# Splitting the first ten weight tiles during the first routing, and subtracting low parts in four pieces

## The chip, the cores and the metric

The kernel runs on one core of a Trainium2 chip. The metric is the time of one execution in microseconds (us); the kernel before takes 1088.62 us in the median of three runs (1088.23 to 1089.11). The engines are named as in the profile: PE (TensorE) multiplies, DVE (VectorE), ACT (ScalarE) and POOL (GpSimd) work elementwise, and SP, ACT and POOL start DMA transfers. Each engine works through its own queue in order.

## The reference, cut to what matters

Three stages follow each other. A linear attention gives 3072 rows of 512 numbers. A router spreads the rows over 8 experts, at most 384 rows each, greedily by score, and each expert is a two-layer network. A last network, the same for all rows, has an ELU between two wide layers:

```python
h = np.maximum(x[mask] @ w1[e], 0.0)      # expert e, 512 -> 1024
out[mask] = h @ w2[e]                     # 1024 -> 512
h = x @ w_in                              # all rows, 512 -> 2048
g = np.where(h > 0.0, h, alpha * (np.exp(np.minimum(h, 0.0)) - 1.0))
return (g @ w_out).astype(np.float32)     # 2048 -> 512
```

## The kernel before

The attention runs first (to about 136 us of the profiled execution). The router then finds the rows of the first expert (phase 0, about 138 to 168 us): a search that goes back and forth between DVE and PE, level after level, since each level's result picks the next level's thresholds. Then the experts follow one by one. Expert n has 8 chunks of L1 and of L2 (its own network) and 16 chunks of F1 and of F2 (the last network on its 384 rows). The order of the chunks is the list `seq`, and `prep` gets a chunk's weights ready three chunks ahead. The router's search for the next expert runs in pieces between them, so DVE's queue in an expert is a fixed mixture of ELU steps, conversions and search steps.

Products are made to full precision from parts: each matrix is a high part (rounded) and a low part (the rest), and three products are added. The tiles of `w_in` and `w_out`, 16 each of 128x512, come as 64-bit numbers. `Wide.chunks` turns each into a 32-bit tile by two DVE operations (L252, L253), an ACT operation (L255) and a POOL addition (L259); `wide.step` runs the next third of that. Thirty such steps run in the attention, which completes ten tiles, w_in and w_out in turn, five of each. The other 22 follow while expert 0 is computed (`CONV`, `n == 0`).

`Wide.parts` gives a chunk's high and low part. On the first call for a tile ACT writes the high part (L272), and POOL subtracts it from the tile (L275: one operation of 128x512), and the low part goes to DRAM through SP's queue (L276); the high part stays on the chip. On later calls the low part is read back by SP (L268). The calls come from `prep`, so all 32 subtractions run in the F1 and F2 chunks of expert 0 (about 216 to 334 us), and experts 1 to 7 only read back. Low parts have three buffers (`LOWS`) for w_in (`wis`) and three for w_out (`wos`); the pools of high parts hand out two spare tiles first and then the tiles of converted weights from the first on, so a high part may wait for an older tile's subtraction.

Of the kernel before, what the change touches and what calls it, by code (L numbers as in the profile page):

```python
# [10 lines left out]
F32 = mybir.dt.float32  # L11
# [189 lines left out]
class Paced:  # L201


    def __init__(self, eng):
        self.eng, self.free, self.now = eng, 0.0, lambda: 0.0
# [13 lines left out]
class Wide:  # L219
# [6 lines left out]
    def __init__(self, nc, tc, ctx, a):  # L226
        self.nc, self.a = nc, a
        self.pools = [ctx.enter_context(tc.tile_pool(name=n, bufs=16 + MORE)) for n in ("win", "wout")]
        self.raw = [[p.tile([128, 512], F32, name="w") for _ in range(16)] for p in self.pools]
        self.low = nc.dram_tensor("low", (2, 16, 128, 512), F32, kind="Internal").ap()  # L230
        self.high = {}
        self.sb = ctx.enter_context(tc.tile_pool(name="wsb", bufs=STAGES))
        self.loaded, self.stage, self.steps = 0, {}, self.chunks()

    def load(self):
# [10 lines left out]
    def chunks(self):  # L246
        V = self.nc.vector
        for i in range(32):
            t = self.stage.pop(i)
            lo, hi = t[:, 0:1024:2], t[:, 1:1024:2]  # L250
            m = self.raw[i % 2][i // 2].bitcast(I32)
            V.tensor_scalar(m, hi, 3, 0x3FFFFFFF, op0=OP.logical_shift_left, op1=OP.bitwise_and)  # L252
            V.scalar_tensor_tensor(m, hi, -0x40000000, m, op0=OP.bitwise_and, op1=OP.bitwise_or)  # L253
            yield
            self.nc.scalar.activation(lo, lo.bitcast(U32), AF.Copy, scale=2.0 ** -29)  # L255
            if i:
                self.load()
            yield
            self.nc.gpsimd.tensor_tensor(m, m, lo, OP.add)  # L259
            yield  # L260

    def parts(self, which, f, pool, later):


        nc, name = self.nc, ("wis", "wos")[which]
        lo = pool.tile([128, 512], F32R, name=name, bufs=LOWS)
        if (which, f) in self.high:
            nc.sync.dma_start(lo.bitcast(F32), self.low[which, f])  # L268
            return self.high[which, f], lo
        hi = self.high[which, f] = self.pools[which].tile([128, 512], F32R, name="w")  # L270
        src = self.raw[which][f]
        nc.scalar.activation(hi, src, AF.Copy)  # L272

        def low():
            nc.gpsimd.tensor_sub(lo, src, hi.bitcast(F32))  # L275
            nc.sync.dma_start(self.low[which, f], lo.bitcast(F32))  # L276

        later(low)
        return hi, lo
# [305 lines left out]
def mlps(nc, tc, ctx, a, xd, out, router, wide, ident, acc, rot, pms):  # L585

    sb = ctx.enter_context(tc.tile_pool(name="sb", bufs=2))
# [6 lines left out]
    def gather_w(n, which, pair):  # L594
        t = sb.tile([128, 1024], F32, name="s" + which)
        nc.gpsimd.indirect_dma_start(  # L596
            out=t, out_offset=None, in_=a[f"{which}_{pair}"],
            in_offset=bass.IndirectOffsetOnAxis(ap=router.es[n][:, :1], axis=0))
        WS[n, which, pair] = t

    def gather_x(n, tb):
        t = sb.tile([128, DM], F32, name="row", bufs=4)
        nc.gpsimd.indirect_dma_start(
            out=t, out_offset=None, in_=xd,
            in_offset=bass.IndirectOffsetOnAxis(ap=router.idx[n][:, tb:tb + 1], axis=0))
        XG[n, tb] = t
# [21 lines left out]
    def tick(us):  # L628

        clock[0] += us  # L630
        while heap and heap[0][0] <= clock[0]:
            heapq.heappop(heap)[2]()
# [155 lines left out]
    def advance(i):  # L788

        while ahead[0] <= min(i, len(seq) - 1):  # L790
            kind = seq[ahead[0]][0]
            if sum(ck[0] == kind for ck in WSP) == ROOM[kind]:
                return
            prep(seq[ahead[0]])
            ahead[0] += 1
# [2 lines left out]
        return acc.tile([128, 512], F32, name="acc")[:, :384]  # L798

    router.spare = spare  # L800
    for _ in router.phase(0):
        tick(1.0)
        if 0 in router.es and (0, "w1", 0) not in WS:
            gather_w(0, "w1", 0)
            gather_w(0, "w2", 0)
        if 0 in router.idx and (0, 0) not in XG:
            for tb in range(3):
                gather_x(0, tb)
            advance(1)
# [45 lines left out]
def body(ctx, tc, a, xd, out):  # L855
# [33 lines left out]
    pms = ctx.enter_context(tc.tile_pool(name="pms", bufs=1, space=PSUM))  # L889

    mlps(nc, tc, ctx, a, xd, out, router, wide, ident, acc, rot, pms)


# [87 lines left out]
```

## Time and profile before

| what | value |
|---|---|
| median of 3 runs | 1088.62 us |
| the profiled execution: its own time | 1088.59 us |
| its span, first to last instruction | 1086.8 us |
| busy: PE, DVE, POOL, ACT | 998.1, 741.5, 406.3, 350.3 us |
| chain that ended last: PE, DVE, the rest | 72%, 18%, 10% |

A page lists for each engine how long it was busy, in which parts of the span, and which group of instructions (a line, an operation, its tiles) cost how much. A table by stretches gives the same for chosen windows of time. A time line gives single instructions with start and duration; behind some of them stands how long the engine had been idle before, and for whom it waited. An instruction's duration holds any time in which it had started but could not get on.

### The profile page before, as it was taken

What the parts mean: (1) busy time and instruction counts of PE and PEld (TensorE: products, weight loads), DVE (VectorE), ACT (ScalarE), POOL (GpSimd) and SP (SyncE); (2) the same over time, 40 slices, a digit from 0 to 9 for tenths busy, and PEclk for the clock granted to TensorE, in tenths of its full rate; (3) what the DMA queues carried; (4) which work ended last, traced back from release to release, by engine and by line L of the source; (5) the groups of instructions that cost most, each with busy time, mean ns of one, the idle gap of its engine ahead of it and who ended that gap; (6) DMA issues with size and microseconds to landing.
All of it is one profiled execution on the core that took longest, in us unless ns stands there. A gap on an engine that the chain in (4) does not pass through costs nothing.

```text
span 1086.8 us, 20264 instructions
## 1 busy us (share of the span) xinstructions
PE 998.1 (92%) x7730; PEld 896.0 (82%) x7730; DVE 741.5 (68%) x2294; ACT 350.3 (32%) x712; POOL 406.3 (37%) x412
## 2 busy tenths in 40 slices
PE   8888947987689999999999999999999999999995
PEld 6877825876578988998899888988998898999994
DVE  4566677989998877887787788777977513431431
ACT  3343403343344323332343233323332332233221
POOL 4555406766666320622071217021702182027001
PEclk9899959888889999999999999999999999999998
DMA  9788506346434263426432633264227426332441
GB/s 366 252 303 299 192 27 205 109 151 203 174 117 146 68 204 118 137 77 213 124 130 68 226 116 115 78 225 123 99 88 225 124 89 203 123 109 87 126 127 49
DMA packets 68194, 163.43 MB, mean 150 GB/s; under 512 B 8832, under 2 KB 15616, under 8 KB 68096
## 3 DMA queue, kind: packets, MB, share of 16 engines
q1 hardware_dynamic: 49712, 99.04, 27.7%
q0 software_dynamic: 13056, 46.14, 12.6%
q10 hardware_dynamic: 5328, 16.94, 4.6%
q8 instruction: 61, 1.00, 0.4%
q14 instruction: 37, 0.30, 0.1%
HBM read 141.13 MB, written 20.97 MB: 149 GB/s over the span
## 4 chain that ended last, share of the span: by engine, by line
PE 72%; DVE 18%; issue 3%; POOL 2%; DMA 2%; ACT 1%; POOLq 0%; ACTq 0%; DVEq 0%
PE pr L670 10%; PE pr L672 10%; PE pr L671 10%; PE acc L748 8%; PE acc L750 7%; PE acc L749 7%; DVE scr L215 3%; PE py L138 3%; PE acc L670 3%; PE acc L671 3%; PE acc L672 3%; PE pq L107 2%; DVE w L253 2%; DVE Tb L215 2%; DVE candf L215 2%
## 5 line engine op out<-in xcount | busy, mean ns | idle before, releaser
L670 PE MATMUL pr<-yh,w 128*128 128x384 f32 x512 | 179.4, 350 | 1.7 <-DVE ni L215 1.1
L672 PE MATMUL pr<-yh,wis 128*128 128x384 f32 x512 | 175.2, 342 | 0.0
L671 PE MATMUL pr<-yl,w 128*128 128x384 f32 x512 | 173.9, 340 | 0.1
L662 POOL TENSOR_TENSOR w1l<-sw,w1h 128x512 fp32r<-128x512 f32 x56 | 73.1, 1305 | 250.0 <-ACT w1h L659 233.3
L748 PE MATMUL acc<-w,gh 128*128 128x512 f32 x384 | 158.1, 412 | 0.0
L750 PE MATMUL acc<-w,gl 128*128 128x512 f32 x384 | 154.0, 401 | 3.3 <-DVE gl L215 3.3
L749 PE MATMUL acc<-wos,gh 128*128 128x512 f32 x384 | 154.2, 402 | 0.0
L596 POOL DMA_INDIRECT sw<-in_w,es x64 | 66.3, 1036 | 190.7 <-DVE es L215 142.3
L736 ACT ACTIVATE gh<-g 128x384 fp32r<-128x384 f32 x128 | 67.2, 525 | 181.5 <-DVE g L215 181.5
L215 DVE TENSOR_SCALAR_CACHE_REDUCE scr<-vt,candf 128x192 bf16<-128x192 f32 x350 | 124.3, 408 | 1.8
L729 ACT ACTIVATE g<-pr 128x384 f32<-128x384 f32 x128 | 62.8, 490 | 181.2 <-PE pr L672 173.1
L215 DVE TENSOR_SCALAR g<-g 128x384 f32<-128x384 f32 x128 | 49.2, 385 | 83.9 <-ACT g L729 82.3
L670 PEld LDWEIGHTS pr<-yh,w 128*128 128x128 f32 x512 | 98.2, 192 | 7.7 <-issue 2.7
L671 PEld LDWEIGHTS pr<-yl,w 128*128 128x128 f32 x512 | 98.1, 192 | 4.5 <-issue 0.4
L672 PEld LDWEIGHTS pr<-yh,wis 128*128 128x128 f32 x512 | 97.8, 191 | 0.0
L215 DVE TENSOR_TENSOR gl<-g,gh 128x384 fp32r<-128x384 f32 x128 | 77.4, 605 | 25.7 <-ACT gh L736 24.4
L750 PEld LDWEIGHTS acc<-w,gl 128*128 128x128 f32 x384 | 73.8, 192 | 22.1 <-DVE gl L215 4.6
L672 PE MATMUL pr<-xh,w1l 128*128 128x384 f32 x256 | 87.1, 340 | 4.0 <-POOL w1l L662 3.9
L670 PE MATMUL pr<-xh,w1h 128*128 128x384 f32 x256 | 88.1, 344 | 1.5 <-ACT w1h L659 1.5
L670 PE MATMUL acc<-hh,w2h 128*128 128x384 f32 x256 | 88.1, 344 | 0.0
L748 PEld LDWEIGHTS acc<-w,gh 128*128 128x128 f32 x384 | 73.6, 192 | 16.1 <-issue 2.4
L671 PE MATMUL acc<-hl,w2h 128*128 128x384 f32 x256 | 86.2, 337 | 0.4 <-DVE hl L215 0.4
(187 smaller groups left out, 2096.1 us busy)
## 6 DMA issues: line engine op xcount, KB each, us to landing
wis<-low SPq DMA_DIRECT2D x112, 256.0 KB
wos<-low SPq DMA_DIRECT2D x112, 256.0 KB, 2.7
Q<-in_kq SPq DMA_DIRECT2D x15, 768.0 KB, 5.8
V<-in_kv SPq DMA_DIRECT2D x15, 768.0 KB, 10.0
stg<-in_w_in ACTq DMA_DIRECT2D x16, 512.0 KB, 3.9
stg<-in_w_out ACTq DMA_DIRECT2D x16, 512.0 KB, 5.5
x_rows<-xs SPq DMA_DIRECT2D x32, 192.0 KB, 8.7
low<-wis SPq DMA_DIRECT2D x16, 256.0 KB, 2.0
```

Source lines behind the costliest of these rows:

```text
L138: nc.tensor.matmul(p[h, pr, :], q[r, n, pr], v[r, n, pr], start=True, stop=True)
L215: return getattr(self.eng, name)(*args, **kw)
L596: nc.gpsimd.indirect_dma_start(out=t, out_offset=None, in_=a[f"{which}_{pair}"], in_offset=bass.IndirectOffsetOnAxis(ap=router.es[n][:, :1 ...
L662: (V if (kind, f) in BYV else nc.gpsimd).tensor_sub(lo, src, hi.bitcast(F32))
L670: nc.tensor.matmul(p, ah, bh, start=first, stop=False)
L671: nc.tensor.matmul(p, ah, bl, start=False, stop=False)
L672: nc.tensor.matmul(p, al, bh, start=False, stop=last)
L729: nc.scalar.activation(g, p, AF.Exp)
L736: at(ELU[0], lambda: nc.scalar.activation(gh, g, AF.Copy))
L748: nc.tensor.matmul(p, gh[:, s], wh, start=f == 0, stop=False)
L749: nc.tensor.matmul(p, gh[:, s], wl, start=False, stop=False)
L750: nc.tensor.matmul(p, gl[:, s], wh, start=False, stop=f == 15)
```

## The change

The converter counts its finished tiles in `wide.done`. In the loop over the first routing, each of the first ten turns calls `parts` for one finished tile, w_in and w_out in turn, and runs its subtraction and its store at once. When expert 0 asks for these ten tiles, `parts` now finds the high part and reads the low part back from DRAM. And every subtraction, early or not, is four POOL operations of 128x128 in place of one of 128x512.

```diff
@@ Wide.chunks
             self.nc.gpsimd.tensor_tensor(m, m, lo, OP.add)
+            self.done = i + 1
             yield
@@ Wide.parts
         def low():
-            nc.gpsimd.tensor_sub(lo, src, hi.bitcast(F32))
+            for c in range(0, 512, 128):
+                s = slice(c, c + 128)
+                nc.gpsimd.tensor_sub(lo[:, s], src[:, s], hi[:, s].bitcast(F32))
             nc.sync.dma_start(self.low[which, f], lo.bitcast(F32))
@@ mlps
     router.spare = spare
+    early = iter(range(wide.done))
     for _ in router.phase(0):
         tick(1.0)
+        i = next(early, None)
+        if i is not None:
+            wide.parts(i % 2, i // 2, sb, lambda low: low())
         if 0 in router.es and (0, "w1", 0) not in WS:
```

PE and DVE get the same rows in the same order as before. Lines behind the insertions move on by one to four (L275 becomes L279, L259 becomes L260, L268 becomes L270, L276 becomes L280).

POOL's queue between the attention's last scaling (`tabk`) and the gathers of expert 0's weights (`es0`), before and after; in a row stand line, operation, what is written and read, and the size:

```order
L259 TENSOR_TENSOR w_88<-w_88,stg_1734 128x512
L115 TENSOR_TENSOR V3_144<-V3_144,tabk_146 64x256 x2
L596 DMA sw1_2560<-in_w1_0,es0_2557 128x1024
L596 DMA sw2_2562<-in_w2_0,es0_2557 128x1024
L603 DMA row_2654<-x_rows,idx0_2652 128x512
```

```order
L115 TENSOR_TENSOR V3_144<-V3_144,tabk_146 64x256 x2
L279 TENSOR_TENSOR wis_2269<-w_68,w_2270 128x128 x4
L279 TENSOR_TENSOR wos_2302<-w_84,w_2303 128x128 x4
L279 TENSOR_TENSOR wis_2313<-w_69,w_2314 128x128 x4
L279 TENSOR_TENSOR wos_2323<-w_85,w_2324 128x128 x4
L279 TENSOR_TENSOR wis_2342<-w_70,w_2343 128x128 x4
L279 TENSOR_TENSOR wos_2375<-w_86,w_2376 128x128 x4
L279 TENSOR_TENSOR wis_2386<-w_71,w_2387 128x128 x4
L279 TENSOR_TENSOR wos_2396<-w_87,w_2397 128x128 x4
L279 TENSOR_TENSOR wis_2411<-w_72,w_2412 128x128 x4
L279 TENSOR_TENSOR wos_2444<-w_88,w_2445 128x128 x4
L600 DMA sw1_2640<-in_w1_0,es0_2637 128x1024
```

Forty pieces now stand between the two, ahead of the gathers.

POOL's queue where expert 0's F1 chunks begin, before and after:

```order
L275 TENSOR_TENSOR wis_3239<-w_68,w_3240 128x512
L275 TENSOR_TENSOR wis_3264<-w_69,w_3265 128x512
L259 TENSOR_TENSOR w_92<-w_92,stg_3143 128x512
L275 TENSOR_TENSOR wis_3306<-w_70,w_3307 128x512
L275 TENSOR_TENSOR wos_3309<-w_84,w_3310 128x512
L259 TENSOR_TENSOR w_77<-w_77,stg_3198 128x512
L275 TENSOR_TENSOR wis_3339<-w_71,w_3340 128x512
```

```order
L260 TENSOR_TENSOR w_92<-w_92,stg_3223 128x512
L260 TENSOR_TENSOR w_77<-w_77,stg_3278 128x512
L260 TENSOR_TENSOR w_93<-w_93,stg_3349 128x512
L260 TENSOR_TENSOR w_78<-w_78,stg_3398 128x512
L279 TENSOR_TENSOR wis_3546<-w_73,w_3547 128x128 x4
L260 TENSOR_TENSOR w_94<-w_94,stg_3446 128x512
L279 TENSOR_TENSOR wis_3632<-w_74,w_3633 128x128 x4
```

The additions of the conversion now stand alone until the sixth tile of w_in (w_73).

SP's queue at the same chunks, before and after (`low` is the copy in DRAM):

```order
L276 DMA low<-wis_3239 128x512
L276 DMA low<-wis_3264 128x512
L276 DMA low<-wis_3306 128x512
L276 DMA low<-wos_3309 128x512
L276 DMA low<-wis_3339 128x512
```

```order
L280 DMA low<-wos_2444 128x512
L270 DMA wis_3319<-low 128x512
L270 DMA wis_3341<-low 128x512
L270 DMA wis_3380<-low 128x512
L270 DMA wos_3382<-low 128x512
L270 DMA wis_3407<-low 128x512
L270 DMA wos_3439<-low 128x512
```

Ten stores moved into the routing, and ten reads stand where they were.

## Rows read from the trace of the kernel before

**Rows 1.** Table by stretches (us): busy time and instructions per engine, PE clock, DMA
```profile
138.30:156.00 17.70, 7.52 (x176) 6.24 (x177) 11.79 (x56) 0.00 (x0) 0.00 (x0) 0.50 0.01 2
172.00:216.00 44.00, 36.98 (x286) 32.98 (x285) 37.05 (x60) 15.04 (x30) 31.43 (x24) 0.92 0.47 156
216.00:254.00 38.00, 33.11 (x195) 27.95 (x193) 32.85 (x64) 17.70 (x35) 23.90 (x18) 0.91 0.48 159
254.00:334.00 80.00, 58.57 (x271) 50.73 (x272) 75.79 (x160) 29.43 (x60) 52.03 (x40) 0.84 0.44 155
453.00:560.00 107.00, 106.00 (x587) 96.26 (x586) 86.18 (x330) 34.33 (x70) 32.82 (x33) 1.00 0.42 133
```

**Rows 2.** Time line: one DVE step with no POOL work beside it
```profile
291.44 0.69 DVE L253 SCALAR_TENSOR_TENSOR w<-stg,w 128x512 int32<-128x512 int32 x1
```

**Rows 3.** Time line: a POOL subtraction and the same DVE step beside it
```profile
296.80 1.49 POOL L275 TENSOR_TENSOR wis<-w 128x512 fp32r<-128x512 f32 x1
297.16 1.68 DVE L253 SCALAR_TENSOR_TENSOR w<-stg,w 128x512 int32<-128x512 int32 x1
```

**Rows 4.** Time line of DVE, 216 to 333: rows stretched beside subtractions
```profile
216.91 1.84 DVE L253 SCALAR_TENSOR_TENSOR w<-stg,w 128x512 int32<-128x512 int32 x1
226.14 1.46 DVE L215 TENSOR_SCALAR g<-g 128x384 f32<-128x384 f32 x1
228.84 3.13 DVE L215 TENSOR_TENSOR cmp<-v,cand 128x372 bf16<-128x372 f32 x2
252.69 1.11 DVE L215 TENSOR_TENSOR tot<-CG,rem 128x8 f32<-128x8 f32 x1
332.34 1.71 DVE L215 TENSOR_TENSOR gl<-g,gh 128x384 fp32r<-128x384 f32 x1
```

**Rows 5.** Time lines of PE and DVE: waits for each other in this stretch
```profile
219.27 0.44 PE L671 MATMUL acc<-hl,w2h 128*128 128x384 f32 x1 [0.42 <-DVE hl L215]
245.43 0.17 DVE L215 TENSOR_REDUCE ni<-pm 128x1 int32<-128x8 f32 x1 [0.68 <-PE pm L401]
```

**Rows 6.** Time lines: POOL operations back to back, and DVE rows beside the smaller ones
```profile
29.17 5.41 POOL L115 TENSOR_TENSOR V<-V,tabk 64x256 f32<-64x256 f32 x8
349.62 1.30 POOL L662 TENSOR_TENSOR w2l<-sw,w2h 128x512 fp32r<-128x512 f32 x1
350.86 1.31 POOL L662 TENSOR_TENSOR w1l<-sw,w1h 128x512 fp32r<-128x512 f32 x1
26.40 0.98 DVE L253 SCALAR_TENSOR_TENSOR w<-stg,w 128x512 int32<-128x512 int32 x1
54.40 0.79 DVE L215 TENSOR_TENSOR cmp<-v,jb 128x186 bf16<-128x186 f32 x1
84.10 0.34 DVE L215 TENSOR_TENSOR cmp<-v,jb 128x186 bf16<-128x186 f32 x1
```

**Rows 7.** Time line of DVE: one level of the search in phase 0
```profile
142.85 0.17 DVE L215 TENSOR_REDUCE ni<-pm 128x1 int32<-128x8 f32 x1 [0.28 <-PE pm L401]
143.28 1.00 DVE L215 TENSOR_TENSOR cmp<-v,cand 128x372 bf16<-128x372 f32 x2
144.39 0.19 DVE L215 TENSOR_TENSOR pre<-jb,Tb 128x31 int32<-128x31 int32 x1
144.85 0.24 DVE L215 TENSOR_SCALAR_CACHE_REDUCE sat<-pm,remp 8x31 bf16<-8x31 f32 x1 [0.28 <-PE pm L395]
145.38 0.17 DVE L215 TENSOR_REDUCE ni<-pm 128x1 int32<-128x8 f32 x1 [0.28 <-PE pm L401]
```

**Rows 8.** Time line of DVE: a step of one number per row, stretched
```profile
350.22 3.22 DVE L215 SCALAR_TENSOR_TENSOR Tb<-ni,Tb 128x1 int32<-128x1 int32 x1
```

**Rows 9.** Time lines of POOL and ACT after phase 0's search; the page's DMA issues
```profile
160.11 1.14 POOL L596 DMA_INDIRECT sw<-in_w,es  x1 [29.68 <-DVE b L215]
164.73 1.15 ACT L659 ACTIVATE w1h<-sw 128x512 fp32r<-128x512 f32 x2 [28.77 <-DVE ga L215]
wos<-low SPq DMA_DIRECT2D x112, 256.0 KB, 2.7
```

More of the change, by code (lines that the diff above doesn't have):

```diff
@@ L232, in __init__ @@
         self.sb = ctx.enter_context(tc.tile_pool(name="wsb", bufs=STAGES))
+        self.done = 0
         self.loaded, self.stage, self.steps = 0, {}, self.chunks()
```

## The prediction

> **What bounds the kernel now.** I read the table by stretches first. From 453 to 560 us, a later expert, PE is busy 106 of 107 us at full clock. Expert 0 is different: from 216 to 334 us DVE is busy 108.6 of 118 us while PE has gaps and a clock of 0.84 to 0.91 [rows 1]. Since PE and DVE wait for each other only in short spells there, whatever makes DVE's queue shorter in this stretch makes the kernel shorter, until PE is next.
>
> The time line then shows that much of DVE's busy time is not work. The step of line L253 takes 0.69 us with POOL quiet [rows 2], and 1.68 us when a subtraction of POOL began just before [rows 3]: 0.99 us are lost, and the step ends 0.55 us after POOL's. DVE steps that read PSUM keep their length beside POOL; those with two inputs on the chip, and plain scalar steps, stretch. I walked through DVE's rows from 216 to 334 us and gave what each takes above its undisturbed length to the POOL operation it overlaps: the 32 subtractions cost DVE about 25.5 us, 0.80 us each (the first and the last such row, and three between, in [rows 4]); POOL's other operations cost some 14 us more. The other place that matters is phase 0. There DVE and PE wait for each other in turn, one level taking 2.53 us [rows 7], and POOL and ACT are idle for 29.68 and 28.77 us before their next work [rows 9].
>
> **The change part by part.** *Ten subtractions leave expert 0.* Beside them stand nine stretched DVE rows, from 216.91 to 252.69 us [rows 4]. Their excess is 1.15, 1.01, 1.12, 0.31, 2.13 (a pair that takes 1.00 undisturbed [rows 7]), 0.53, 0.64, 0.33 and 0.94, together 8.16 us. Not all of it arrives. The first row holds up PE by 0.42 us only [rows 5], so 0.73 of it is swallowed by PE's own run of L2. From 238 to 246 us DVE waits three times, 1.63 us together, the longest 0.68 us for PE [rows 5]; these waits grow first. I take 8.16 - 0.73 - 1.63 = 5.8 us as the gain; the ends are 3 us, if the waits take up about half of the rest as well, and all 8.2 us.
>
> *Forty pieces enter phase 0.* Cost of a piece on POOL: eight operations of 256 columns take 5.41 us, 0.68 each, and one of 512 columns follows the next by 1.24 us [rows 6]. So 256 columns are 0.56 us, and a piece of 128 takes 0.40 us; four take 1.60 in place of 1.24. How long a piece stops a DVE step is not in the trace. An operation of 512 stopped one for 0.99 us [rows 2, 3]; one of 256 stopped a step for 0.45 us (0.79 against 0.34) and another for 0.29 (0.98 against 0.69) [rows 2, 6]. The line through 0.99 and 0.45 gives 0.18 us at 128; a quarter of 0.99 is 0.25. I take 0.18, since the two smaller rows lie below proportion on average.
>
> In those rows with 256 columns DVE came in between two operations of a run, so I let a piece and a DVE step take turns. A level has five steps that a piece can stop: `cand`, two `cmp`, `Tb` and `pre`. DVE has no such step from the end of `pre` (144.58) to the end of the next `ni` (145.55), which takes two or three pieces free of charge; one piece before each of the five steps makes 7.5 per level. On the path lie `cand` and both `cmp`, 3 x 0.18 = 0.54 us. Pieces before `Tb` and `pre` push `sat` by 0.36 less the 0.28 us that it waits for PE anyway [rows 7], 0.08. So a level costs 0.62 us. The first level has four such steps on the path, 0.72 us, and takes about eight pieces; the other 32 need 4.3 levels, 2.7 us. Phase 0 grows by 3.4 us. From below: the pieces stop DVE for at most 40 x 0.18 = 7.2 us in all, and DVE is idle 5.9 of 17.7 us [rows 1], which leaves 1.3. From above with 0.25: 4 x 0.25 + 4.3 x (0.75 + 0.22) = 5.2 us.
>
> POOL should be through by about 157 us, ahead of the gather that comes at 160.11 and moves later by the same 3.4 us [rows 9]. If the pieces ran past it, every microsecond would delay the first weights.
>
> *22 subtractions are cut in four.* They keep 17.3 us of the 25.5, 0.79 each, which is 80% of the 0.99 that a full stop costs. Four pieces stop DVE for 4 x 0.18 x 0.8 = 0.58 us: 22 x 0.21 = 4.6 us gained. Against that, five of the 22 follow directly on a gather of POOL, and the DVE step that met the gather lost the whole run behind it; the run is now 0.36 us longer, 1.8 us. Net gain 2.8 us. Ends: at 0.25 per piece the cut gains nothing and costs the 1.8; if pieces meet a step that they can stop only half the time, it gains 22 x (0.79 - 0.36) = 9.5 less 1.8.
>
> *At nothing:* ten rounding steps of ACT move from a stretch in which it is busy 17.7 of 38 us [rows 1] into its idle time. Ten stores of SP move into phase 0, and ten reads of the same size take their place; a read lands in 2.7 us [rows 9], is queued three chunks ahead, and experts 1 to 7 live on such reads. In SP's queue the stores of later tiles now stand behind reads that wait for a free buffer; what those stores hold up is the buffer of the third tile after. If that cover went, F1 would wait up to 2.7 us for a tile. POOL's extra 22 x 0.36 = 7.9 us fall into a stretch where it is busy 52 of 80 [rows 1].
>
> **Sum.** 1088.59 us of the profiled execution (the median is 1088.62) + 3.4 - 5.8 - 2.8 = 1083.4 us.
>
> **The rivals.** *A, no change.* A piece costs 0.25. Then phase 0 grows by 5.2, the cut gains 0 and gives back 1.8, and 5.8 are saved: 1089.8 us. For it speaks that the step at 54.40 lost 0.45 of a pitch of 0.68, about the same share as at 512; against it the 0.29.
>
> *B, slower.* The port that both need is held for the whole reading of a piece, 0.28 us by the slope in [rows 6]. Place: the search of phase 0, where each of the three steps of a level waits for one piece. Price: 4 x 0.28 + 4.3 x (0.84 + 0.28) = 5.9 us there, 22 x (0.90 - 0.79) = 2.4 and 1.8 in expert 0, less 5.8: 1092.9 us. It decides from about 0.25 us per piece on.
>
> *C, slower by more.* The four pieces of a run don't let DVE in. One row looks like this: a step on one number per row took 3.22 us [rows 8], through three operations of POOL that stood back to back, two of them in [rows 6]. Then phase 0 grows by 40 x 0.40 - 5.9 = 10.1 us, and each kept tile costs 0.36 x 0.8 more, 6.3 us: 1099.2 us. Against it: at 216.91 DVE came in between two subtractions that stood back to back.
>
> *D, the whole piece.* A piece stops DVE for its whole 0.40 us. Phase 0: 4 x 0.40 + 4.3 x (1.20 + 0.52) = 9.0; expert 0: 22 x (1.28 - 0.79) + 1.8 = 12.6; less 5.8: 1104.4 us. The Trainium skill has this as a rule (SBUF — State Buffer, Who interferes with whom): whichever of the two starts first keeps the shared pair of ports for its whole instruction, and the other blocks. The trace agrees that the loser waits, but not on the length: 0.99 of 1.24 us and 0.45 of 0.68, so it has a small chance.
>
> *E, faster by more.* All 8.2 us arrive, phase 0 grows by 1.3, and the cut gains 9.5 - 1.8: 1074.0 us. For it: fewer gaps would also raise PE's clock, 0.84 from 254 to 334 us [rows 1].
>
> **How the numbers follow.** Chances: forecast 0.50 (its own range 1080 to 1086), A 0.22, B 0.10, C 0.06, D 0.03, E 0.09. The range from 1077 to 1094 us holds the forecast, A and B and leaves out C, D and E, 0.18. About 0.2% (2.2 us) is what a measurement of this kernel can tell from no change: faster is the forecast and E, 0.59; the same is A, 0.22; slower are B, C and D, 0.19.
>
> **What would show it right or wrong.** In the profile of the changed kernel: a level of the search of 3.0 to 3.3 us while POOL's pieces run, and 2.5 after them; phase 0's first gather 3 to 4 us later than 160.11; DVE rows of L253 beside pieces below 1.1 us on average; the stretch from the first L1 product to the last F2 product of expert 0 shorter by 8 to 9 us; later experts at 107 us as before. It is wrong if the level grows by over 1 us (B, C, D), if the pieces are still running when the gather is due, if DVE rows are stopped through whole runs of pieces (C), or if PE waits for a low part that comes from DRAM.

## The result, and the profile after

The changed kernel takes 1076.47 us in the median of four runs (1072.23 to 1078.40), the kernel before 1088.42 beside it. The ratio is 0.9891, 95% interval 0.9855 to 0.9927: 11.9 us faster, where 5.2 us were forecast. Two repetitions on other occasions gave 0.9897 (0.9860 to 0.9933) and 0.9874 (0.9843 to 0.9906). The profiled execution took 1078.40 us, its span is 1076.6 us.

The table by stretches of the changed kernel comes first, to be set against [rows 1]: length, busy time and instructions of PE, PE's weight loads, DVE, ACT and POOL, then PE's granted clock, DMA share and GB/s.

```profile
138.20:159.40 21.20, 7.68 (x175) 6.25 (x176) 17.21 (x56) 2.87 (x6) 19.61 (x40) 0.53 0.31 120
178.00:221.80 43.80, 36.51 (x274) 32.96 (x273) 34.51 (x59) 14.40 (x28) 27.54 (x22) 0.88 0.42 143
221.80:252.50 30.70, 29.64 (x193) 25.86 (x192) 25.24 (x60) 12.62 (x25) 12.32 (x14) 1.00 0.47 147
252.50:323.80 71.30, 54.99 (x271) 47.28 (x270) 67.31 (x160) 28.38 (x58) 61.46 (x96) 0.90 0.51 173
442.80:549.80 107.00, 106.00 (x587) 96.26 (x586) 86.18 (x330) 34.30 (x70) 32.83 (x33) 1.00 0.42 133
```

Later experts are as before: 106.00 of 107 us of PE in the last row, to the digit, and from the first output row of expert 0 to the end both kernels take 747.6 us. All of the difference lies in front of that. In the stretch that held 195 products in 38 us there are now 193 in 30.7, with PE busy 29.6 of them. In the next one, 271 products took 80 us and take 71.3. DVE has the same 160 instructions there, and 67.31 us in place of 75.79. POOL, with 61.46 of 71.3 us, has little room left.

To see where each microsecond went I cut every trace at the same six rows. These are the time lines' rows of the changed kernel: the last product of the attention, POOL's first gather for expert 0, the first `hh` of L1, the first and the sixth ELU step `g` of F1, and the first output row of expert 0.

```profile
135.93 0.64 PE L171 MATMUL pL<-wg,xT 128*64 128x8 f32 x16 [0.18 <-ACT xT L162]
162.82 1.13 POOL L600 DMA_INDIRECT sw<-in_w,es  x1 [4.69 <-DVE pos L215]
178.45 0.49 ACT L688 ACTIVATE hh<-pr 128x384 fp32r<-128x384 f32 x1 [2.43 <-PE pr L676]
230.29 0.49 ACT L733 ACTIVATE g<-pr 128x384 f32<-128x384 f32 x1 [1.05 <-PE pr L676]
251.25 0.49 ACT L733 ACTIVATE g<-pr 128x384 f32<-128x384 f32 x1
329.01 0.59 ACT L761 ACTIVATE row<-acc 128x512 f32<-128x512 f32 x1
```

The same rows in the kernel before; its first gather starts at 160.11 us [rows 9]:

```profile
136.01 0.64 PE L171 MATMUL pL<-wg,xT 128*64 128x8 f32 x16 [0.18 <-ACT xT L162]
175.05 0.49 ACT L684 ACTIVATE hh<-pr 128x384 fp32r<-128x384 f32 x1 [2.43 <-PE pr L672]
225.18 0.49 ACT L729 ACTIVATE g<-pr 128x384 f32<-128x384 f32 x1
252.77 0.47 ACT L729 ACTIVATE g<-pr 128x384 f32<-128x384 f32 x1
339.19 0.59 ACT L757 ACTIVATE row<-acc 128x512 f32<-128x512 f32 x1
```

The stages between these rows, for all kernels of the study (experiments below), stand in the next table in us. The ratio sets a kernel against executions of the kernel before beside it. Gains in us below are this ratio times the time of the kernel before, about 1086 us; plain differences of the medians depart from them by up to 2.4 us.

| kernel | last pL to gather | gather to first hh | first hh to g 1 | g 1 to g 6 | g 6 to output row | ratio to before |
|---|---|---|---|---|---|---|
| before | 24.10 | 14.94 | 50.13 | 27.59 | 86.42 | 1 |
| changed | 26.89 | 15.63 | 51.84 | 20.96 | 77.76 | 0.9891 |
| changed, repeated | 26.84 | 15.70 | 48.67 | 20.94 | 77.75 | 0.9897 |
| changed, third time | 26.86 | 15.60 | 51.84 | 20.96 | 77.85 | 0.9874 |
| e1, move, no cut | 30.77 | 15.74 | 50.38 | 22.63 | 85.75 | 1.0001 |
| e3, move, cut in phase 0 alone | 26.84 | 15.75 | 49.50 | 22.62 | 85.83 | 0.9975 |
| e4, move, cut in expert 0 alone | 30.78 | 15.73 | 48.82 | 20.94 | 77.85 | 0.9919 |
| e2, cut, no move | 24.08 | 15.01 | 49.61 | 24.51 | 78.82 | 0.9919 |
| e2, repeated | 24.06 | 15.11 | 49.75 | 24.52 | 78.00 | 0.9876 |
| two pieces | 26.66 | 15.76 | 51.77 | 21.78 | 81.76 | 0.9932 |
| eight pieces | 26.89 | 15.78 | 49.43 | 20.94 | 84.69 | 0.9991 |
| additions cut too | 26.88 | 15.82 | 51.95 | 20.04 | 80.80 | 0.9902 |
| attention's additions cut | 26.69 | 15.88 | 51.57 | 20.94 | 77.82 | 0.9876 |
| no subtraction of the 22 | 26.86 | 15.70 | 51.68 | 20.94 | 64.85 | 0.9754 |

Three of the five columns repeat to 0.3 us where the program is the same there, and the column behind g 6 to 0.1 us in the changed kernel and to 0.8 in e2. So one profile of each kernel is enough to read them. The column from the first hh to g 1 doesn't repeat: 51.84, 48.67 and 51.84 us for one program. Nor does the end of the attention, which lay between 131.8 and 138.9 us in the 14 profiles. These two are large enough for most of the 6 to 10 us by which single executions differ, and no difference in them is ascribed to the change. For the end of the attention this was tried (below). For the other column it is open: six of the nine profiles with pieces in phase 0 have 51.6 to 52.0 us there, the other five profiles 48.8 to 50.4.

From the kernel before to the changed one the table says: +2.8 and +0.7 up to the first hh, -6.6 from g 1 to g 6, -8.7 behind it; together -11.8 us, close to the 11.9 us of the medians. The two profiled executions themselves differ by 10.2 us, since the changed one took 1.7 us more from the first hh to g 1.

### The profile page after: what moved, and what is told of

The parts are those of the page before. It is cut to its first block, busy times and chain, and to the rows that moved or that the text cites. A ratio compares the mean times of both kernels' runs of the same rounds, so it can differ in the third digit from the quotient of the medians.

```text
span 1076.6 us, 20354 instructions
## 1 busy us (share of the span) xinstructions
PE 992.8 (92%) x7730; PEld 891.6 (83%) x7730; DVE 732.7 (68%) x2294; ACT 350.5 (33%) x712; POOL 424.3 (39%) x508
## 4 chain that ended last, share of the span: by engine, by line
PE 71%; DVE 19%; issue 3%; POOL 3%; DMA 2%; ACT 1%; another core or an unknown queue 0%; POOLq 0%; SPq 0%; DVEq 0%; ACTq 0%
PE pr L674 10%; PE pr L676 10%; PE pr L675 10%; PE acc L752 8%; PE acc L753 7%; PE acc L754 7%; DVE scr L215 3%; PE acc L674 3%; PE acc L675 3%; PE acc L676 3%; PE py L138 2%; DVE Tb L215 2%; PE pq L107 2%; DVE g L215 2%; DVE candf L215 2%
## 5 line engine op out<-in xcount | busy, mean ns | idle before, releaser
L215 DVE TENSOR_SCALAR g<-g 128x384 f32<-128x384 f32 x128 | 52.6, 411 | 84.8 <-ACT g L733 84.0
L215 DVE TENSOR_TENSOR gl<-g,gh 128x384 fp32r<-128x384 f32 x128 | 74.0, 578 | 25.6 <-ACT gh L740 24.4
L675 PE MATMUL pr<-xl,w1h 128*128 128x384 f32 x256 | 87.3, 341 | 0.3 <-DVE xl L215 0.3
L676 PE MATMUL acc<-hh,w2l 128*128 128x384 f32 x256 | 85.9, 336 | 0.0
```

Of the source, the lines that this page charges most:

```text
L215: return getattr(self.eng, name)(*args, **kw)
L675: nc.tensor.matmul(p, ah, bl, start=False, stop=False)
L676: nc.tensor.matmul(p, al, bh, start=False, stop=last)
```

## The experiments

**The change once more**, beside the next three kernels.

> The changed kernel itself, on the chip and beside the runs of the next three. Its four runs lay between 1072.2 and 1078.4 us, against 1088.4 for the kernel before. Theory T (short pieces stop VectorE less, above all in the tiles that stay in expert 0) and rival M (the move of the ten tiles brings all of it) expect the same here: 10 to 16 us below the kernel before.

Measured: 1076.48 us, ratio 0.9897, 11.2 us faster, as both expected.

**e1: the move without the cut.** Against the changed kernel:

```diff
-            for c in range(0, 512, 128):
-                s = slice(c, c + 128)
-                nc.gpsimd.tensor_sub(lo[:, s], src[:, s], hi[:, s].bitcast(F32))
+            nc.gpsimd.tensor_sub(lo, src, hi.bitcast(F32))
```

> The first ten tiles are split during phase 0 as in the changed kernel, but every subtraction is one operation of 512 columns, in phase 0 and in expert 0. Theory T (the cut is worth about 9 us in the kept part, the move about 6.6, phase 0 pays): 6.6 us gained up to g row 6, nothing behind it, and phase 0 longer by 3 to 8 us, since one whole subtraction can stop a step for 0.99 us and about 1.5 of them fall into a level; so 3.6 us faster to 1.4 us slower than before. Rival M (the move alone brings it, in a lighter queue of POOL and SP): 8 to 12 us faster.

Measured: 1087.64 us, ratio 1.0001 (0.9982 to 1.0020). The move alone brings nothing: 7.5 us more up to the first hh use up the 5.0 us that it saves between g 1 and g 6 and the 0.7 behind it. Rival M falls.

**e3: pieces in phase 0, whole subtractions in expert 0.**

```diff
-            for c in range(0, 512, 128):
-                s = slice(c, c + 128)
+            n = 128 if which + 2 * f < 10 else 512
+            for c in range(0, 512, n):
+                s = slice(c, c + n)
```

> Ten tiles in phase 0 in four pieces, the 22 that stay in expert 0 in one operation of 512 columns each. Theory T: the gain behind g row 6 goes; phase 0 +3.5, up to g row 6 -6.6, behind it 0: about 3 us faster than before (0 to 5). Rival M: as the changed kernel, 10 us faster or more.

Measured: 1084.74 us, ratio 0.9975 (0.9962 to 0.9987), 2.7 us faster, where theory T said 3. Behind g 6 it is back at 85.83 us.

**e4: the other half.** The same edit with `n = 512 if which + 2 * f < 10 else 128`.

> Ten tiles in phase 0 in one operation of 512 columns each, the 22 that stay in four pieces. Theory T: phase 0 +3 to +8 in place of +3.5, then -6.6 and -8.7 as in the changed kernel: 7 to 12 us faster than before, level with the changed kernel or up to 5 us behind it. Rival M: the same as the run without any cut.

Measured: 1079.27 us, ratio 0.9919 (0.9896 to 0.9941), 8.8 us faster. The four kernels add up. The cut in expert 0 is worth 8.5 us beside pieces in phase 0 (0.9975 to 0.9897) and 8.9 beside whole operations there (1.0001 to 0.9919); pieces in phase 0 are worth 2.4 and 2.8.

**e2: the cut without the move.**

```diff
-    early = iter(range(wide.done))
+    early = iter(())
```

> No tile is split in phase 0: all 32 stay in expert 0, each subtraction in four pieces. From the first four runs: pieces in place of whole ones for the 22 kept tiles were worth 8.5 us (0.9975 to 0.9897). Theory T (each piece stops VectorE less than its share of a whole operation, wherever it stands): 8.5 us for the 22, and about 0.2 to 0.4 us for each of the ten others, 2 to 4 us; nothing is paid in phase 0: 10 to 12 us faster than before, level with the changed kernel. Rival M (the cut pays only because the move emptied POOL's queue in the first part of expert 0): at most 6 us faster, with g row 6 no earlier than before.

Measured: 1075.85 us, ratio 0.9919 (0.9894 to 0.9944), 8.8 us faster; the repetition below gave 0.9876, 13.5 us. T had said 10 to 12, which lies between the two, and rival M at most 6. Its column from g 1 to g 6 is 3.1 us shorter than before and 3.6 longer than in the changed kernel. So the cut does not need the move; what the move is worth beside it was tried again below.

**Two pieces, and eight.** `n = 128 if which + 2 * f < 10 else 256`, then `else 64`.

> As the changed kernel, but the 22 tiles that stay in expert 0 are subtracted in two pieces of 256 columns. Theory T with a stop that falls faster than the piece (a whole subtraction costs VectorE 0.86 us in this stretch, a piece of 128 costs 0.164; the line through both gives 0.39 for 256): 0.79 per tile in place of 0.66, so about a third of the 8.5 us is kept: 5 to 6 us faster than before. Rival S (what counts is only that VectorE gets in between at all, so the first cut brings most): 8 to 10 us faster than before.

Measured: 1079.73 us, ratio 0.9932 (0.9905 to 0.9960), 7.4 us faster. T had said 5 to 6 and rival S 8 to 10; the interval holds both. Behind g 6 the stage is 81.76 us, half way between the whole operation and four pieces.

> As the changed kernel, but the 22 tiles that stay are subtracted in eight pieces of 64 columns. Theory T without another bound: 8 x 0.05 = 0.40 us per tile in place of 0.66, 15 to 17 us faster than before. Rival P (POOL becomes the bound: it is busy 63.1 of 73 us with pieces of 128, and eight pieces of about 0.4 us take 1 us more per tile, 20 us in this stretch): later than the changed kernel, between 3 us faster and 8 us slower than before, with POOL busy through the stretch and TensorE waiting for low parts.

Measured: 1084.25 us, ratio 0.9991 (0.9972 to 1.0010): nothing left, as rival P said. The table by stretches, from g 6 to the output row, tells why; columns as above. This is e3, with whole operations:

```profile
252.62:338.45 85.83, 64.28 (x301) 55.09 (x300) 81.42 (x185) 31.20 (x65) 52.31 (x40) 0.86 0.47 162
```

The changed kernel, with pieces of 128:

```profile
251.25:329.01 77.76, 61.45 (x301) 52.90 (x300) 73.63 (x180) 31.55 (x66) 64.96 (x100) 0.91 0.52 176
```

Eight pieces of 64:

```profile
248.69:333.38 84.69, 64.56 (x300) 51.91 (x299) 67.05 (x184) 31.73 (x65) 80.43 (x181) 0.90 0.45 155
```

And the kernel without subtractions of the 22 tiles, which comes at the end of this section:

```profile
251.50:316.35 64.85, 58.19 (x301) 50.75 (x300) 59.47 (x184) 41.72 (x85) 24.36 (x20) 0.95 0.61 212
```

With eight pieces DVE is relieved by another 6.6 us, to 67.05, but POOL is busy 80.43 of 84.69 us. The list of waits shows the change of the bound: whom PE waited for, in total, how often, and the longest wait. First e3:

```profile
PE pm L423 <- DVE vm L215: 6.8, 1, 6.8
PE pm L567 <- DVE ohp L215: 6.6, 3, 3.0
PE pm L452 <- DVE scr L215: 5.6, 3, 2.3
PE pm L534 <- DVE CG L215: 1.4, 1, 1.4
```

The same list with eight pieces:

```profile
PE acc L754 <- POOL wos L280: 11.7, 8, 3.2
PE pm L567 <- DVE ohp L215: 5.1, 2, 2.8
```

In e3 PE waits for DVE alone. With eight pieces it waits eight times, 11.7 us, for a low part that POOL has not finished. The list of groups gives POOL's price of a piece there: two rows of 64-column subtractions.

```profile
L280 POOL TENSOR_TENSOR wos<-w 128x64 fp32r<-128x64 f32 x88 | 30.5, 378 | 0.1
L280 POOL TENSOR_TENSOR wis<-w 128x64 fp32r<-128x64 f32 x72 | 25.7, 388 | 0.8 <-PE acc L754 0.7
```

A piece of 64 takes POOL 0.38 us there, so eight take 3.06. Four of 128 take 2.17 in the changed kernel (0.54 each on average), and a whole subtraction took 1.36 (27.3 us for 20, before).

**The additions cut as well.** Against the changed kernel:

```diff
-            self.nc.gpsimd.tensor_tensor(m, m, lo, OP.add)
+            for c in range(0, 512, 128):
+                s = slice(c, c + 128)
+                self.nc.gpsimd.tensor_tensor(m[:, s], m[:, s], lo[:, s], OP.add)
```

> The changed kernel with the additions of the conversion (512 columns, one per tile) cut into four pieces as well, in attention and in expert 0. Beside the ten additions in the F part of expert 0 VectorE loses 7.0 us in the changed kernel, 0.7 each. Theory T: the same cut saves 20 to 30% of it, 1.5 to 2 us there and as much in the part before: 1 to 4 us faster than the changed kernel. Rival P (POOL, busy 63.1 of 73 us, becomes the bound: 0.6 to 0.9 us more per tile): the same as the changed kernel or up to 6 us slower.

Measured: 1074.91 us, ratio 0.9902 (0.9873 to 0.9930), the same as the changed kernel, as rival P allowed; the gain of T is not there. Behind g 6 it is 3.0 us longer: POOL is busy 71.7 of 80.8 us, and PE waits 4.3 us for low parts, in three waits that the changed kernel does not have. There the cut has run into POOL's own limit. In this profile 0.9 us less from g 1 to g 6 and an attention that ended at 131.8 us stand against that. Whether the cut shortens the attention was asked with the next kernel.

**The additions cut in the attention alone**, `n = 128 if i < 10 else 512` in that loop; beside it the changed kernel a third time and e2 again.

> The changed kernel with the additions of the ten tiles converted during attention in four pieces; those of expert 0 stay whole. With all 32 in pieces, expert 0 behind g row 6 was 3.0 us longer and the total was level, and attention ended at 131.8 us against 133.8 to 138.9 in nine other profiles. Theory A (attention got shorter by the cut): 2 to 4 us faster than the changed kernel. Rival B (the end of attention only varied, as it does between runs of one kernel): within 1.5 us of the changed kernel.

> The changed kernel once more, on the same chip as the next three, so that they can be set against it. By its eight runs so far: 8 to 14 us below the kernel before.

> The cut without the move once more, beside the changed kernel. By stages in the profiles so far the move, with pieces, costs 3.5 us up to the first product of L1, wins 3.6 between g rows 1 and 6 and 1.1 behind it. Theory N (the move is worth next to nothing once the subtractions are cut): 0 to 2 us slower than the changed kernel. Rival M (the move still brings most of what it brought on paper, 5.8 less 3.4): 2.4 us or more slower.

Measured: 1076.24 us (0.9876, 0.9850 to 0.9902) for the attention's additions, 1075.01 us (0.9874) for the changed kernel and 1075.11 us (0.9876, 0.9850 to 0.9902) for e2, as rival B and theory N said. The attention's additions make no difference; its end at 131.8 us is within the variation. And the cut alone is level with the whole change: the move of ten tiles is worth nothing that this measurement can tell, once the subtractions are cut. By the stages it costs 3.3 to 3.5 us up to the first hh, wins 3.6 from g 1 to g 6 and 0.1 to 1.1 behind it.

**No subtraction for the 22.** ScalarE copies the tile into the low part's place, so the low parts of these tiles are not computed.

```diff
+            if which + 2 * f >= 10:
+                nc.scalar.activation(lo, src, AF.Copy)
-            for c in range(0, 512, 128):
+            for c in range(0, 512 if which + 2 * f < 10 else 0, 128):
```

> The changed kernel, but for the 22 tiles that stay in expert 0 the low part is not computed: ScalarE writes a second copy of the tile in its place, and POOL has no subtraction there. Theory T (the stops of VectorE by the pieces, 13.5 us in the profile behind g row 6 and some 1 us before, lie on the path): 9 to 14 us faster than the changed kernel. Rival Q (most of what is left is covered by TensorE or by ScalarE, which gets 13 us more work): at most 5 us faster.

Measured: 1063.23 us, ratio 0.9754 (0.9723 to 0.9785), 11.8 us below the changed kernel beside it, where T had said 9 to 14 and rival Q at most 5. Behind g 6 the stage is 64.85 us in place of 77.85. In a walk through DVE's rows (told in the next section) the time above undisturbed length falls from 22.8 to 7.0 us, 15.8 less, and the stage is 13.0 shorter. So with room on POOL, about four fifths of what POOL takes from DVE there lies on the path. No version that computes all low parts beats the changed kernel clearly; this run shows what a way of forming the low parts that does not stop DVE would be worth.

## Why the prediction was right on the move and wrong on the cut

**Phase 0: right, with some luck.** Forecast +3.4 us up to the first gather; measured +2.8 there. Another 0.7 came behind it, which the working has no term for. It belongs to the move (e2 has 0.1 there), and no run shows where it comes from. POOL's time line shows the pieces through before the gather at 162.82 us; the first and the last of ten runs of four:

```profile
138.52 1.71 POOL L279 TENSOR_TENSOR wis<-w 128x128 fp32r<-128x128 f32 x4 [8.18 <-ACT w L274]
...
156.44 1.70 POOL L279 TENSOR_TENSOR wos<-w 128x128 fp32r<-128x128 f32 x4
```

The forecast said 157 us, and they ended at 158.1. One level on DVE, to be read against [rows 7]:

```profile
146.90 0.17 DVE L215 TENSOR_REDUCE ni<-pm 128x1 int32<-128x8 f32 x1 [0.28 <-PE pm L405]
147.10 0.19 DVE L215 SCALAR_TENSOR_TENSOR cand<-ni,pre 128x31 int32<-128x31 int32 x1
147.32 1.44 DVE L215 TENSOR_TENSOR cmp<-v,cand 128x372 bf16<-128x372 f32 x2
148.68 0.40 DVE L215 SCALAR_TENSOR_TENSOR Tb<-ni,Tb 128x1 int32<-128x1 int32 x1
149.12 0.41 DVE L215 TENSOR_TENSOR pre<-jb,Tb 128x31 int32<-128x31 int32 x1
149.46 0.23 DVE L215 TENSOR_SCALAR_CACHE_REDUCE sat<-pm,remp 8x31 bf16<-8x31 f32 x1
149.97 0.17 DVE L215 TENSOR_REDUCE ni<-pm 128x1 int32<-128x8 f32 x1 [0.28 <-PE pm L405]
```

A level takes 3.07 us, against 2.53 before and 3.15 in the sum. The pair of `cmp` lost 0.44 us (0.36 forecast for both), `Tb` about 0.25 and `pre` 0.22, so a step that met a piece lost more than the 0.18 taken. `cand` lost nothing, where 0.18 was taken, and `sat`'s wait of 0.28 us for PE is gone, as in the working. The level came out close because these misses pull opposite ways. With whole operations in the same place (e1) the two `cmp` of one level take 3.06 us, and the stage 6.7 us more than before to the gather:

```profile
143.08 3.06 DVE L215 TENSOR_TENSOR cmp<-v,cand 128x372 bf16<-128x372 f32 x2
```

**Ten subtractions leave expert 0: right.** Forecast -5.8 us. In e1 and e3, which have this and no cut in expert 0, g 1 to g 6 is 5.0 us shorter and the stage behind it 0.6 or 0.7: 5.6. PE's granted clock rose there as well, from 0.88 to 1.00, but it does not set this stage's length: the two profiles of e2 have 24.51 us at 0.93 and 24.52 at 1.00.

**At nothing: right.** The reads from DRAM took the place of the subtractions with no wait in the list of PE, and POOL's extra time stayed under its cover. That cover was thinner than I put it: a run of four took 2.0 us in phase 0 (20.0 us for ten), not 1.60, and POOL went from 52 of 80 to 61 of 71 us. The runs with eight pieces and with cut additions show it gone.

**Cutting the 22: the step that failed.** Forecast -2.8 us net, from -4.6 for shorter stops and +1.8 for runs behind gathers. From e3 to the changed kernel the stage behind g 6 shrinks by 8.1 us and the one before it by 1.7, 9.7 together by the table, 8.5 by the runs. DVE's busy time behind g 6 falls by 7.8, from 81.42 to 73.63 us, and its idle time stays at 4.4 and 4.1: the gain is DVE's own. PE's granted clock in this stage rose too, from 0.84 before and 0.86 in e3 to 0.91, as rival E expected, but the stage does not follow it. These are the changed kernel's two repetitions, at 0.89 and 0.93, to be set against its 77.76 us at 0.91 above:

```profile
247.64:325.39 77.75, 63.10 (x301) 54.64 (x300) 73.62 (x180) 31.31 (x65) 64.92 (x100) 0.89 0.53 176
248.15:326.00 77.85, 60.19 (x301) 51.57 (x300) 73.70 (x180) 31.54 (x66) 65.03 (x100) 0.93 0.54 176
```

Walking through DVE's rows behind g 6 and giving what each takes above its undisturbed length to the POOL operations beside it, by how long they overlap, I find there (the changed kernel in its three profiles):

| what the stops stand beside | e3 | changed |
|---|---|---|
| subtractions (20 tiles) | 17.3 us | 13.5 to 13.9 us |
| additions (whole in both) | 9.5 us | 6.7 to 7.0 us |
| POOL's other operations | 3.0 us | 2.1 to 2.2 us |
| sum | 29.8 us | 22.7 to 22.8 us |

Only the sum is free of the rule of sharing. If a step's loss goes whole to the operation that overlaps it longest, the subtractions fall from 21.3 to 11.7 us and the additions rise from 7.1 to 9.2. The run without the 22 subtractions gives their price with no such rule. From g 1 to the output row DVE loses 35.5 us in e3, 27.0 in the changed kernel and 11.4 without them. So a whole subtraction costs DVE 1.10 us with all that follows from it, and a cut one 0.71, where the forecast had 0.79 and 0.58. The cut saves 0.39 us per tile in place of 0.21, which makes 8.5 us for 22 tiles in place of 4.6.

The 1.8 us that the forecast took off again did not come: these 8.5 us hold the runs behind gathers. Two rows of DVE behind gathers in the changed kernel:

```profile
266.83 3.32 DVE L253 TENSOR_SCALAR w<-stg 128x512 int32<-128x512 int32 x1
270.79 2.11 DVE L215 TENSOR_SCALAR g<-g 128x384 f32<-128x384 f32 x1
```

And one of e3, from the same time line:

```profile
273.03 1.72 DVE L215 TENSOR_SCALAR g<-g 128x384 f32<-128x384 f32 x1
```

The same step g loses 1.77 us in place of 1.38 behind a gather: the price of 0.36 us per run was right. But only three runs were lost whole in the changed kernel, five in e3, as other steps now stood at the gathers. Which step stands at a gather was not forecast; that it came out this way is luck.

The prediction took each subtraction's stop by itself, and let everything else that POOL does cost DVE the same as before. One place shows how that can fail. These are three DVE steps in e3, two of the conversion and one of ELU, and the POOL operations beside them:

```profile
276.69 1.46 DVE L253 TENSOR_SCALAR w<-stg 128x512 int32<-128x512 int32 x1
278.18 1.68 DVE L254 SCALAR_TENSOR_TENSOR w<-stg,w 128x512 int32<-128x512 int32 x1
279.78 1.46 DVE L215 TENSOR_SCALAR g<-g 128x384 f32<-128x384 f32 x1
276.49 1.36 POOL L280 TENSOR_TENSOR wos<-w 128x512 fp32r<-128x512 f32 x1 [1.97 <-ACT w L274]
277.81 1.49 POOL L260 TENSOR_TENSOR w<-w,stg 128x512 int32<-128x512 int32 x1
279.27 1.76 POOL L280 TENSOR_TENSOR wis<-w 128x512 fp32r<-128x512 f32 x1
```

The same steps in the changed kernel:

```profile
274.84 0.60 DVE L253 TENSOR_SCALAR w<-stg 128x512 int32<-128x512 int32 x1
275.48 0.84 DVE L254 SCALAR_TENSOR_TENSOR w<-stg,w 128x512 int32<-128x512 int32 x1
276.24 0.62 DVE L215 TENSOR_SCALAR g<-g 128x384 f32<-128x384 f32 x1
274.65 2.52 POOL L279 TENSOR_TENSOR wos<-w 128x128 fp32r<-128x128 f32 x4 [1.97 <-ACT w L274]
```

With whole operations DVE and POOL take turns, one step for one operation: each step that gets free meets the next operation that POOL has in its queue, a subtraction, an addition, a subtraction. The three steps take 4.55 us. With pieces all three get through beside a single run of four, in 2.02 us, and are done before POOL begins the addition. So here the cut saves the stop beside the operation that stands behind the subtraction as well. That this order of events is behind each microsecond of the 8.5 is read from such places and was not tried by itself.

**The price of a stop by size: close.** Per operation DVE lost, by the sharing above, 0.865 us beside 512 columns (e3), 0.38 beside 256, 0.17 beside 128 and 0.054 beside 64. Less the run without subtractions, from g 1 on, it is 1.10, 0.46, 0.18 and 0.05. A piece of 128 was taken at 0.18 x 0.8 = 0.14 on average. Rival A's price of 0.25 for a piece that meets a step is as near as 0.18 in phase 0 (0.22 to 0.25). What fails in A is what it made of it: no gain from the cut, where 8.5 us came, and 0.97 us more per level, where 0.54 came. Rivals B and D needed 1.1 and 1.7 us per level, and C falls since DVE comes in between the pieces of a run, except behind gathers. The Trainium skill (SBUF — State Buffer, Who interferes with whom) has it that the loser stays out for the other's whole instruction: the trace agrees that it waits, but a piece occupied POOL for about 0.43 us (1.70 for four) and cost DVE 0.17 to 0.18 on average.

**The range.** Its lower end of 1077 us missed the median by 0.5. Rival E came nearest in time, 1074.0, but not by its steps: phase 0 grew by 3.5 us, not 1.3, and the early tiles gave 5.6, not 8.2. Its gain from the cut ended at 7.7 us net, since only the cut operations' own stops were in that bound.

## What to carry to other kernels

When two engines get in each other's way, price a shorter operation by what the other engine can do in the gaps, not only by its own shorter stop: a step that slips through can also miss the next operation in the queue. The best size is where one engine's relief meets the other's overhead, here 128 columns: 256 left half of the gain, and 64 made POOL the bound. And before moving work into an idle engine's time, look at who waits for whom there: POOL was idle in phase 0, but DVE was on the path, and the move paid back what it brought.

## What the runs showed of the hardware

- A POOL subtraction costs DVE on average less than in proportion to its columns: 1.10, 0.46, 0.18 and 0.05 us at 512, 256, 128 and 64, against the run without subtractions.
- POOL pays for it: four pieces of 128 take 1.70 us undisturbed and 2.52 with three DVE steps let through; with DVE steps in between, a piece of 64 took 0.38 us on average and one of 128 took 0.54, so halving the piece saved POOL less than a third of its time.
- Behind an indirect DMA of POOL the turns can fail. In three of six such places of the changed kernel the DVE step that met the DMA stayed out through the whole run of pieces behind it, once through the addition behind that as well (the row at 266.83, 3.32 us in place of 0.40).
